# One decode step of a transformer block, forward and backward: q kept as rows, a fifth V tile, and the last head up to d(o) in another order

## The chip, the cores and the metric

The kernel runs on one core of a Trainium2 chip. The core has a matrix engine (PE), a vector engine (DVE), a scalar engine (ACT), a general engine (POOL), a sync engine (SP) and 16 DMA engines that move data between the device memory (HBM) and the on-chip memory (SBUF, 128 partitions; matmul results go to PSUM). The metric is the time of one execution on the device in microseconds (us); a kernel's figure is the median of its runs.

## The reference, cut

Inputs are bf16. One token x (1 x 640) goes through an attention block with a cache of 8192 keys and values for each of 32 heads (head size 192), and then through an MLP; both blocks are modulated by a condition c. The kernel must give the output and the gradients with respect to x, k_cache, v_cache, wq, wo, w3, w4, c and w_mod.

```python
def A(x, k_cache, v_cache, wq, wo):
    q = (x @ wq).reshape(1, 1, 32, 192).transpose(0, 2, 1, 3)
    scores = einsum('bhqd,bhkd->bhqk', q, k_cache) * 192 ** -0.5
    p = softmax(scores)
    o = einsum('bhqk,bhkd->bhqd', p, v_cache)
    return o.transpose(0, 2, 1, 3).reshape(1, 1, 6144) @ wo
def B(x, w1, w2, w3, w4):
...
    x1 = x + hs
    return x1 + gelu(layernorm(x1) @ w3) @ w4
sa, ca, ga, sb, cb, gb = (silu(c) @ w_mod).reshape(6, 640)
h = layernorm(x) * (1 + ca) + sa
x = x + ga * A(h, k_cache, v_cache, wq, wo)
h = layernorm(x) * (1 + cb) + sb
out = x + gb * B(h, w1, w2, w3, w4)
```

With a sequence of one token, hs (a mixer over shifted positions) is zero, so B is the MLP with its residual. k_cache and v_cache are 32 x 8192 x 192 each, that is 3 MB per head and cache; their gradients dK and dV have the same size. In the backward pass, d(o) is the gradient at the attention's output of each head; dV is p times d(o), and dK is dS times q, where dS = p * (V·d(o) - a constant of the head).

## The kernel before, in words

**Data.** A half head of K or V is one tile of 128 partitions x 32 positions x 192 (1536 KB). There are five K tiles, with names KX, KY, KC, KD, KE for the last ones in use (L348 to L353), and three V tiles, VB (L321). The queue of SP issues the loads: `load_k` L360, `load_v` L324, `load_w` L195 (wq and w_mod), `load_wo` L200 (one pair of heads of wo, 480 KB), `load_rows` L652 (rows of w4). The queue of POOL issues the stores. The order of the instructions on PE, DVE, ACT and SP is the order in which the program writes them (`manual_schedule`, L515 and L986).

**First phase, L516 to L600: heads 0 to 30, pipelined.** The vector q of every head, broadcast over the partitions and scaled, stands in one tile `qs_bc` (128 x 6144, L252). For head i, DVE multiplies K by q (L330) and adds the halves of the product (L334), PE sums the rest with identity matmuls (`dot_tree` L336), DVE reduces to the scores S (L344); then softmax (L365, E is the exponential), and E times V into tiles `vs` of a quarter head (L380 on DVE, L387 on ACT; three buffers). PE makes M = K-transposed times (E V), from which the gradient of q comes later, and the sums of o, in quarters (`m_quarter` L417, its units in `m_units` L396: 16 "main" matmuls for the first 128 columns of K and 16 "rest" for the other 64). For each pair of heads, `pair_sums` L471, `pair_o` L479 and `pair_ao` L488 make the pair's share of the attention output.

**Between the phases, L605 to L956.** An order written out by hand: the scores of the last head 31 (`score_mul`, `score_tree`), o of head 30 (`o_rows` L424, 64 matmuls) and the four quarters of its M between other work (`vs_act` L647, `vs_dve` L638 for E V), the last two pairs, the second layernorm by six sums (`S6` L766, two rsqrt L772 and L785, `n2_bf` L790), u = n2 w3 (`ups` L821), the gelu and its derivative, `du_bf` L869. In the same stretch PE transposes w3 in nine groups (`w3t` L813; a PSUM buffer of two, an ACT copy L808 each), and wo of the last pair in two (`do_t` L899, copies L895). Then `h2` L905 (g w4), `dn_ps` L916 (du w3T), `pr` L935, four means, and `dao_bf` L953, the gradient at the attention's output. The rows of w4 are in `w4b` and in `KX` (loads L666, L730, L765); the first six rows of the gradient of w4 are staged in KX (L934, L955) and stored from there (L956). `vs3`, the quarter of E V for the last M quarter, is made on ACT alone.

**Second phase, from L978: 64 half heads, from head 31 down.** `do_mm` L1011 makes `do_r`, d(o) of a head (matmuls with the transposed wo, then an ACT activation L1021). For each half head s, DVE multiplies V by d(o) (`mul_q` L1036), PE sums (`tree_q` L1051), DVE makes dS, PE and ACT make dV (`dv_groups` L1058, with E rows from `load_er` L990), and DVE makes dK = dS times q (`dk_part` L1070, with q as a slice of qs_bc, L1365). Both are stored. The V tiles come from a ring `v_buf` L1290; the load of half head s + 4 is issued in step s (L1405). The output tiles come from a ring `OB` L354. Beside it run the gradients of wq, wo, w_mod and w3 (`g_dq`, `g_dwo`, `g_wm`, `g_dw3`), in slots between the steps.

```python
353:    KX, KY, KC, KD, KE = (KB[(2 * HQ + k) % NKB] for k in (-4, -5, -3, -2, -1))
354:    OB = (KC, VB[2], KX, KE, KD)
1028:    wo_l[TL - 1] = load_wo(TL - 1)
1029:    er_l = {0: load_er(0, nc.sync), 1: load_er(1, nc.sync)}
1291:        return KY if s == 0 else VB[2] if s == 1 else (VB[1], KY, VB[0])[s % 3]
1365:        qh = qs_bc[:, h * DH : (h + 1) * DH]
1404:        if 0 < s < NS - 4:
1405:            v_l[s + 4] = load_v(*ht(s + 4), v_buf(s + 4))
```

## Time and profile before

| | before |
|---|---|
| median of 3 runs | 1406.0 us (1405.18 to 1406.44) |
| profiled execution, device time | 1404.99 us |
| its span (first to last instruction) | 1403.2 us |
| PE busy | 1182.8 us (84%), 12680 matmuls |
| DVE busy | 1111.0 us (79%) |
| ACT busy | 903.2 us (64%) |
| POOL busy | 104.9 us (7%) |
| DMA | 569.36 MB, mean 406 GB/s |
| mean granted clock of PE | 0.722 |

The profile of one execution is a page with the busy time of each engine, the span in 40 equal slices (each digit is the busy share of a slice in tenths, 9 is 90% or more), the DMA queues, the groups of instructions and the chain of work that ended last. Further views cut a stretch of time into windows (busy time of each engine, number of instructions in brackets, the clock that PE was granted, the share of time in which the 16 DMA engines were busy, and GB/s), or list the instructions of one engine in order of time (start, length, line, operation, what is written from what is read, and in brackets the idle time just before and what ended it). A line such as "L1072 DVE ... VB<-qs_bc,dS" is line 1072 of the kernel, on DVE, writing a VB tile from qs_bc and dS. The largest groups are the tree sums of V·d(o) on PE (L1056, 379.9 us), the copies of dV on ACT (L1068, 321.5 us with output tiles among the K tiles) and E V on ACT (L387, 303.6 us); 60% of the DMA time is on the queue of SP and 38.5% on that of POOL.

### The profile page before, as it was taken

To read this page: it belongs to the slowest core of one execution; us is meant where nothing else is said; L and a number is where in the kernel's file an instruction comes from. 1 tells how busy PE (TensorE), PEld (TensorE's weight loads), DVE (VectorE), ACT (ScalarE), POOL (GpSimd) and SP (SyncE) were. 2 spreads that over 40 slices of the span, in tenths; PEclk is the share of its full clock that TensorE was granted. 3 is DMA by queue.
4 is the path that set the end of the run, shared out by engine and by line. 5 is a ranking of instruction groups with operands and counts; after the bars stand their busy time and mean duration, and the time that the engine had idled before them with its cause. 6 is when DMAs were issued, how large, how long until landed. Compare 5 with 4: busy or idle time off the path is not lost.

```text
span 1403.2 us, 30406 instructions
## 1 busy us (share of the span) xinstructions
PE 1182.8 (84%) x12680; PEld 744.5 (53%) x12680; DVE 1111.0 (79%) x1460; ACT 903.2 (64%) x1972; POOL 104.9 (7%) x190
## 2 busy tenths in 40 slices
PE   3889889999998999899867987888989788779975
PEld 2777777777777778543323443434444344334421
DVE  4989899999999998976765875776766777868775
ACT  0777777777777778666554665665656476546654
POOL 0000000000000000110110110101110111101110
PEclk9999999999999999655555555555555565555555
DMA  9999999999999997699999999999999999999998
GB/s 375 401 417 419 415 417 423 407 424 409 422 414 415 408 413 306 223 394 425 423 396 421 423 422 421 421 424 422 425 418 425 423 413 423 421 412 398 426 379 367
DMA packets 76184, 569.36 MB, mean 406 GB/s; under 512 B 7278, under 2 KB 25022, under 8 KB 35982
## 3 DMA queue, kind: packets, MB, share of 16 engines
q1 hardware_dynamic: 51162, 342.03, 59.8%
q0 software_dynamic: 24368, 224.87, 38.5%
q8 instruction: 99, 1.62, 0.4%
q10 hardware_dynamic: 516, 0.51, 0.1%
q14 instruction: 39, 0.32, 0.1%
HBM read 340.95 MB, written 226.43 MB: 404 GB/s over the span
## 4 chain that ended last, share of the span: by engine, by line
issue 42%; DVE 21%; DMA 17%; PE 11%; POOL 5%; ACT 1%; SPq 0%; POOLq 0%; DVEq 0%
DMA KB<-in_A_k_cache_dram 10%; DVE prod L330 8%; DVE prod L334 4%; PE mp L402 3%; DMA out_dram<-KB 3%; DVE vs L380 2%; POOL out_dram L1322 2%; PE half_ps L340 2%; POOL out_dram L1318 2%; DMA w_st<-in_A_wq_dram 2%; PE mp L407 2%; DVE pq L1037 2%; DMA wo_st<-in_A_wo_dram 1%; PE dot_ps L1056 1%; DMA out_dram<-VB 1%
## 5 line engine op out<-in xcount | busy, mean ns | idle before, releaser
L1056 PE MATMUL dot_ps<-pq,ident_bf 128*128 128x256 bf16 x1494 | 379.9, 397 | 18.4 <-DVE dP L344 16.3
L1068 ACT CAST KB<-dv_ps 128x768 bf16<-128x768 f32 x416 | 321.5, 803 | 108.6 <-PE dv_ps L1067 106.3
L387 ACT ACTIVATE vs<-VB,Ef 128x192 bf16<-128x192 bf16 x840 | 303.6, 447 | 0.0
L1072 DVE TENSOR_TENSOR KB<-qs_bc,dS 128x3072 bf16<-128x3072 bf16 x98 | 169.4, 1753 | 103.5 <-DMA out_dram<-KB 91.8
L1056 PEld LDWEIGHTS <-ident_bf 128*128 128x128 bf16 x1494 | 150.1, 124 | 173.4 <-issue 134.3
L1067 PE MATMUL dv_ps<-do_r,er_b 1*128 1x192 bf16 x2048 | 230.3, 337 | 4.3 <-ACT KB L1068 2.9
L330 DVE TENSOR_TENSOR prod<-KB,qs_bc 128x6144 bf16<-128x6144 bf16 x62 | 207.9, 3353 | 28.1 <-DMA KB<-in_A_k_cache_dram 21.5
L402 PE MATMUL mp<-vs,KB 128*128 128x193 bf16 x1984 | 189.3, 247 | 4.6 <-ACT vs L387 3.4
L402 PEld LDWEIGHTS <-KB 128*128 128x128 bf16 x1984 | 169.0, 97 | 13.6 <-DMA KB<-in_A_k_cache_dram 5.3
L895 ACT COPY wT<-wT_ps 128x1024 bf16<-128x1024 bf16 x82 | 79.0, 964 | 128.7 <-PE wT_ps L894 128.5
L1037 DVE TENSOR_TENSOR pq<-VB,do_r 128x3072 bf16<-128x3072 bf16 x86 | 150.5, 1749 | 12.7 <-PE dot_ps L1056 12.7
L1067 PEld LDWEIGHTS <-er_b 1*128 1x128 bf16 x2048 | 69.3, 104 | 154.8 <-issue 152.2
L340 PE MATMUL half_ps<-prod,ident_bf 128*128 128x256 bf16 x744 | 95.1, 279 | 45.7 <-DVE prod L334 45.5
L380 DVE TENSOR_TENSOR vs<-VB,E 128x1728 bf16<-128x1728 bf16 x120 | 123.7, 1052 | 0.3 <-ACT vs L387 0.3
L334 DVE TENSOR_TENSOR prod<-prod 128x3072 bf16<-128x3072 bf16 x62 | 108.8, 1754 | 1.0
L340 PEld LDWEIGHTS <-ident_bf 128*128 128x128 bf16 x744 | 73.0, 99 | 64.1 <-issue 55.0
L407 PE MATMUL mp<-vs,KB 128*64 128x193 bf16 x1976 | 106.5, 250 | 0.0
L1068 ACT CAST VB<-dv_ps 128x768 bf16<-128x768 f32 x96 | 75.1, 802 | 39.3 <-PE dv_ps L1067 39.1
L367 ACT ACTIVATE E<-S_h,negm 128x256 bf16<-128x256 f32 x31 | 15.8, 508 | 116.9 <-DVE negm L538 114.6
L407 PEld LDWEIGHTS <-KB 128*64 128x64 bf16 x1976 | 79.4, 110 | 19.8 <-issue 19.5
L344 DVE TENSOR_REDUCE dP<-dot_ps 128x32 f32<-128x512 f32 x64 | 44.0, 687 | 57.8 <-PE dot_ps L1056 57.6
L1072 DVE TENSOR_TENSOR VB<-qs_bc,dS 128x3072 bf16<-128x3072 bf16 x30 | 51.5, 1753 | 29.5 <-DMA out_dram<-VB 24.8
(360 smaller groups left out, 1132.7 us busy)
## 6 DMA issues: line engine op xcount, KB each, us to landing
VB<-in_A_v_cache_dram SPq DMA_DIRECT2D x103, 1536.0 KB
out_dram<-KB POOLq DMA_DIRECT2D x99, 1536.0 KB, 16.2
KB<-in_A_k_cache_dram SPq DMA_DIRECT2D x64, 1536.0 KB
...
```

The costliest lines, as they stand in the source:

```text
L330: V_.tensor_tensor(out=prod, in0=src, in1=vec[:, None, :].to_broadcast([P, JH, DH]), op=ALU.mult)
L334: V_.tensor_tensor(out=prod[:, :, 0:HW], in0=prod[:, :, 0:HW], in1=prod[:, :, DH - HW : DH], op=ALU.add)
L340: T_.matmul(ps, lhsT=ident_bf, rhs=prod[:, :, k : k + TF], start=(k == 0), stop=(k == w - TF))
L380: V_.tensor_tensor(out=vs[:, 0:n, 0:DH].rearrange("p j (a b) -> p j a b", b=4), in0=v[:, v0 : v0 + n, :].rearrange("p j (a b) -> p j a b", ...
L387: A_.activation(out=vs[:, k, 0:DH], in_=v[:, v0 + k, :], func=ACT.Copy, scale=Ef[:, j0 + k : j0 + k + 1])
L402: T_.matmul(mp[:, 0:MW], lhsT=kb[:, j0 + k, 0:P], rhs=vs[:, k, 0:MW], start=(q == 0 and k == 0), stop=(z and k == JQ - 1), skip_group_chec ...
L407: T_.matmul(mp[p0 : p0 + 64, MO : MO + MW], lhsT=kb[:, j0 + k, P:DH], rhs=vs[:, k, 0:MW], start=False, stop=(z and k >= JQ - 2), skip_grou ...
L1037: V_.tensor_tensor(out=pq[:, q], in0=v_l[s][:, q * JQ : (q + 1) * JQ, :], in1=do_of(ht(s)[0])[:, None, :].to_broadcast([P, JQ, DH]), op=AL ...
L1056: T_.matmul(ps[:, q * JQ : (q + 1) * JQ, :], lhsT=ident_bf, rhs=pq[:, q, :, k : k + TS], start=(k == 0), stop=(k == w - TS), skip_group_ch ...
L1067: T_.matmul(ps[:, b, k * DH : (k + 1) * DH], lhsT=er[p0 : p0 + 1, 2 * m + k, :], rhs=doh[p0 : p0 + 1, :], start=True, stop=True)
L1068: A_.copy(out=dV4[:, 2 * q : 2 * q + 2, m * PW : (m + 1) * PW], in_=ps[:, :, 0:PW])
L1072: V_.tensor_tensor(out=dK[:, lo:hi, :].rearrange("p j (a b) -> p j a b", b=4), in0=qh.rearrange("p (a b) -> p a b", b=4)[:, None, :, :].to ...
```

## The change

**q as rows.** At head 28, POOL's queue stores row 0 of qs_bc (all heads' q, 12 KB) to a DRAM tile `q_d`, and at head 30 loads it back as `q_rows`, 32 rows x 192. In the second phase, a new function `q_bc(h)` broadcasts one row with a one-hot matmul into PSUM and copies it to a small tile `qh` on ACT: once before the loop for head 31, and then at the end of each head's last step for the next head. The tile qs_bc is free after the last head's scores. It then holds rows 4 to 12 of w4 (one load instead of two into KX), stages the first six rows of w4's gradient, and takes KX's place in the ring of output tiles (as `QT`).

**A fifth V tile.** KX becomes a V tile: half head 4 of the second phase is loaded into it (`v4`) after the rest of M quarter 1. The ring `v_buf` has four tiles, and step s issues the load of half head s + 5.

**The last head up to d(o) in another order.** `o_rows` of head 30 is split around the row maximum of the last scores. The matmuls of pair 14 (`pair_ao`) and the load of the last row block of w3 go behind the exponential. All of vs2 is made on ACT; vs3 is made on ACT (0 to 8) and DVE (8 to 16, behind du). `m_main` and `m_rest` take the place of m_units. The first w3 transposes come behind u's matmuls. The M quarters stand at other places in the order; the second half of quarter 3 comes behind `pr`, with `m_add` of head 30 behind `dao_bf`.

**wo ahead of h2.** `do_t` of the last pair comes before h2's matmuls; its result goes to the tile of w3's last row block (`w3_w`) instead of a part of KC. The load of wo for pair 14 goes from before the loads of E's rows to behind the second `do_mm`. The copy of h2 to `bo` and the first six gradient rows of w4 go behind `dao_bf`: three on ACT, three on DVE. A few small temporary tiles now share buffers (tag "rows").

The diff, without context (the hunks that only give the small tiles the shared tag are left out):

```diff
...
@@ -252,0 +253,3 @@
+QT = qs_bc.rearrange("p (j d) -> p j d", d=DH)
+q_rows = const.tile([HQ, DH], BF16, name="q_rows")
+q_d = dram.tile([HQ, DH], BF16, name="q_d")
@@ -354 +357 @@
-OB = (KC, VB[2], KX, KE, KD)
+OB = (KC, VB[2], QT, KE, KD)
@@ -410,0 +414,5 @@
+def m_main(q, kb, vs, mp, lo, hi):
+    j0 = (q % 2) * JQ
+    for k in range(lo, hi):
+        T_.matmul(mp[:, 0:MW], lhsT=kb[:, j0 + k, 0:P], rhs=vs[:, k, 0:MW], start=(q == 0 and k == 0), stop=(q == 3 and k == JQ - 1), skip_group_check=True)
@@ -424 +432 @@
-def o_rows(h, v2, op):
+def o_rows(h, v2, op, lo=0, hi=J):
@@ -426 +434 @@
-    for j in range(J):
+    for j in range(lo, hi):
@@ -586,0 +595,4 @@
+        if i == H1 - 3:
+            nc.gpsimd.dma_start(out=q_d.rearrange("h d -> (h d)").rearrange("(o n) -> o n", o=1), in_=qs_bc[0:1, :])
+        if i == H1 - 1:
+            nc.gpsimd.dma_start(out=q_rows, in_=q_d)
@@ -679,2 +690,0 @@
-    op_y = psO.tile([P, 256], FP32, name="op")
-    o_rows(H1 - 1, vy, op_y)
@@ -689,0 +700,2 @@
+    op_y = psO.tile([P, 256], FP32, name="op")
+    o_rows(H1 - 1, vy, op_y, 0, JH)
@@ -690,0 +703,2 @@
+    mx = row_max(x["S"])
+    o_rows(H1 - 1, vy, op_y, JH, J)
@@ -694,8 +707,0 @@
-    ps_ao = pair_ao(o2, wo_l.pop(TL - 1), psB, "b")
-    w3_4 = wst.tile([P, F], BF16, name="w3_4", tag="wo")
-    nc.sync.dma_start(out=w3_4, in_=w3d[:, 4, :])
-    V_.tensor_copy(out=AO[:, :, 2 * TL - 2 : 2 * TL], in_=ps_ao)
-    pe = m_units(0, ky[0], vs0, mp)
-    pe.pop(0)()
-    mx = row_max(x["S"])
-    pe.pop(0)()
@@ -707,2 +712,0 @@
-    A_.activation(out=zy, in_=es0, func=ACT.Copy, scale=32.0)
-    A_.copy(out=oy, in_=op_y[:, 0:DH])
@@ -710,0 +715,7 @@
+    A_.activation(out=zy, in_=es0, func=ACT.Copy, scale=32.0)
+    A_.copy(out=oy, in_=op_y[:, 0:DH])
+    ps_ao = pair_ao(o2, wo_l.pop(TL - 1), psB, "b")
+    w3_w = wst.tile([P, 3 * D], BF16, name="w3_w", tag="wo")
+    w3_4 = w3_w[:, 0:F]
+    nc.sync.dma_start(out=w3_4, in_=w3d[:, 4, :])
+    load_rows(qs_bc[:, 0 : 8 * D], 4, 12)
@@ -712,0 +724 @@
+    vs_dve(vs1, 1, 0, JQ // 2)
@@ -716 +727,0 @@
-    vs_dve(vs1, 1, 0, JQ // 2)
@@ -717,0 +729 @@
+    V_.tensor_copy(out=AO[:, :, 2 * TL - 2 : 2 * TL], in_=ps_ao)
@@ -719,3 +731 @@
-    vs_act(vs2, 2, JQ // 2, JQ // 2 + 3)
-    vs_dve(vs2, 2, 0, JQ // 2)
-    pe.pop(0)()
+    vs_act(vs2, 2, 0, 2)
@@ -723 +733 @@
-    vs_act(vs2, 2, JQ // 2 + 3, JQ)
+    vs_act(vs2, 2, 2, 12)
@@ -726 +735,0 @@
-    m_rest(0, ky[0], vs0, mp, JQ // 2, 13)
@@ -729,2 +738 @@
-    m_rest(0, ky[0], vs0, mp, 13, JQ)
-    load_rows(flat(KX)[:, 0 : 4 * D], 4, 8)
+    m_main(0, ky[0], vs0, mp, 0, 5)
@@ -746,5 +754 @@
-    vs3 = new_vs(3)
-    vs_act(vs3, 3, 0, 8)
-    pe = m_units(1, ky[0], vs1, mp)
-    pe.pop(0)()
-    pe.pop(0)()
+    m_main(0, ky[0], vs0, mp, 5, JQ)
@@ -763,3 +767,4 @@
-    pe.pop(0)()
-    pe.pop(0)()
-    load_rows(flat(KX)[:, JQ * DH : JQ * DH + 4 * D], 8, 12)
+    m_rest(0, ky[0], vs0, mp, 0, JQ)
+    m_main(1, ky[0], vs1, mp, 0, JQ)
+    m_rest(1, ky[0], vs1, mp, 0, JQ)
+    v4 = load_v(H1 - 2, 0, KX)
@@ -781 +786,3 @@
-    vs_act(vs3, 3, 8, 10)
+    vs_act(vs2, 2, 12, JQ)
+    vs3 = new_vs(3)
+    vs_act(vs3, 3, 0, 2)
@@ -817,4 +823,0 @@
-    w3t()
-    pe = m_units(2, ky[1], vs2, mp)
-    pe.pop(0)()
-    pe.pop(0)()
@@ -830 +833 @@
-    vs_act(vs3, 3, 10, 14)
+    w3t()
@@ -850,3 +853 @@
-    vs_act(vs3, 3, 14, JQ)
-    pe.pop(0)()
-    pe.pop(0)()
+    m_main(2, ky[1], vs2, mp, 0, 8)
@@ -853,0 +855,2 @@
+    m_main(2, ky[1], vs2, mp, 8, JQ)
+    vs_act(vs3, 3, 2, 8)
@@ -855,2 +858 @@
-    pe = m_units(3, ky[1], vs3, mp)
-    pe.pop(0)()
+    m_rest(2, ky[1], vs2, mp, 0, JQ)
@@ -859 +860,0 @@
-    pe.pop(0)()
@@ -871 +872 @@
-    pe.pop(0)()
+    m_main(3, ky[1], vs3, mp, 0, 8)
@@ -873 +874 @@
-    pe.pop(0)()
+    m_rest(3, ky[1], vs3, mp, 0, 8)
@@ -875 +875,0 @@
-    mt = mp_out(H1 - 1, mp)
@@ -901 +901 @@
-            woT[t] = flat(KC)[:, JQ * DH : JQ * DH + 3 * D] if t == TL else bst.tile([P, 15 * P], BF16, name="wT", tag="wT")
+            woT[t] = w3_w if t == TL else bst.tile([P, 15 * P], BF16, name="wT", tag="wT")
@@ -905,4 +904,0 @@
-    h2_ps = psB.tile([P, 512], FP32, name="h2_ps", tag="b")
-    for k in range(ND):
-        for a in range(NF):
-            T_.matmul(h2_ps[:, k : k + 1], lhsT=w4r(a)[:, k * P : (k + 1) * P], rhs=g_bf[:, a : a + 1], start=(a == 0), stop=(a == NF - 1))
@@ -910,0 +907,8 @@
+    h2_ps = psB.tile([P, 512], FP32, name="h2_ps", tag="b")
+    def h2_part(lo, hi):
+        for k in range(lo, hi):
+            for a in range(NF):
+                T_.matmul(h2_ps[:, k : k + 1], lhsT=w4r(a)[:, k * P : (k + 1) * P], rhs=g_bf[:, a : a + 1], start=(a == 0), stop=(a == NF - 1))
+    h2_part(0, ND)
@@ -921 +925 @@
-    m_add(H1 - 1, mp, mt)
+    vs_dve(vs3, 3, 8, JQ)
@@ -933,5 +936,0 @@
-    V_.tensor_copy(out=bo, in_=h2_ps[:, 0:ND])
-    dw4_dve(flat(KX), 0, 0, 3)
-    pr = col(4 * ND, "pr").rearrange("p (a b) -> p a b", b=ND)
-    V_.tensor_tensor(out=pr, in0=dn_ps[:, None, :].to_broadcast([P, 4, ND]), in1=G, op=ALU.mult)
-    ps = mean_mm(pr.rearrange("p a b -> p (a b)"), 4 * ND)
@@ -943,0 +943,7 @@
+    V_.tensor_tensor(out=Bg, in0=B1, in1=ga, op=ALU.mult)
+    pr = col(4 * ND, "pr").rearrange("p (a b) -> p a b", b=ND)
+    V_.tensor_tensor(out=pr, in0=dn_ps[:, None, :].to_broadcast([P, 4, ND]), in1=G, op=ALU.mult)
+    ps = mean_mm(pr.rearrange("p a b -> p (a b)"), 4 * ND)
+    m_main(3, ky[1], vs3, mp, 8, JQ)
+    m_rest(3, ky[1], vs3, mp, 8, JQ)
+    mt = mp_out(H1 - 1, mp)
@@ -946 +951,0 @@
-    V_.tensor_tensor(out=Bg, in0=B1, in1=ga, op=ALU.mult)
@@ -955,2 +960,5 @@
-    dw4_dve(flat(KX), 0, 3, 6)
-    dw4_store(flat(KX), 0, 6)
+    V_.tensor_copy(out=bo, in_=h2_ps[:, 0:ND])
+    dw4_act(qs_bc, 0, 0, 3)
+    dw4_dve(qs_bc, 0, 3, 6)
+    m_add(H1 - 1, mp, mt)
+    dw4_store(qs_bc, 0, 6)
@@ -1028 +1035,0 @@
-wo_l[TL - 1] = load_wo(TL - 1)
@@ -1069,0 +1077,7 @@
+def q_bc(h):
+    ps = psB.tile([P, 512], FP32, name="q_ps", tag="b")
+    T_.matmul(ps[:, 0:DH], lhsT=pick(HQ, h), rhs=q_rows, start=True, stop=True)
+    qh = bst.tile([P, DH], BF16, name="qh", bufs=2)
+    A_.copy(out=qh, in_=ps[:, 0:DH])
+    return qh
...
@@ -1291 +1305 @@
-return KY if s == 0 else VB[2] if s == 1 else (VB[1], KY, VB[0])[s % 3]
+return KY if s == 0 else VB[2] if s == 1 else (VB[0], VB[1], KX, KY)[(s - 2) % 4]
@@ -1295 +1309,2 @@
-v_l = {s: v_buf(s) for s in range(4)}
+v_l = {s: v_buf(s) for s in range(5)}
+assert ht(4) == (H1 - 2, 0) and v_buf(4) is KX
@@ -1331,0 +1347 @@
+wo_l[TL - 1] = load_wo(TL - 1)
@@ -1334 +1350 @@
-v_l[4] = load_v(*ht(4), v_buf(4))
+v_l[5] = load_v(*ht(5), v_buf(5))
@@ -1358,0 +1375 @@
+qh = q_bc(H1)
@@ -1365 +1381,0 @@
-qh = qs_bc[:, h * DH : (h + 1) * DH]
@@ -1404,2 +1420,2 @@
-if 0 < s < NS - 4:
-    v_l[s + 4] = load_v(*ht(s + 4), v_buf(s + 4))
+if 0 < s < NS - 5:
+    v_l[s + 5] = load_v(*ht(s + 5), v_buf(s + 5))
@@ -1444,0 +1461,2 @@
+if nxt and ht(s + 1)[0] != h:
+    qh = q_bc(ht(s + 1)[0])
```

## The prediction

> **What bounds the kernel now.** All times are us from the start of the one profiled execution: span 1403.2, device time 1404.99, so 1.8 lies around the span; the median of the runs is 1406.0, 1.0 above it. I read the 40 slices first, and then the hole they show in windows of 5 us (columns: length, busy time of PE, PEld, DVE, ACT, POOL, granted PE clock, DMA share, GB/s).
>
> ```profile
> DMA  9999999999999997699999999999999999999998
> 0.00:540.00 540.00, 473.91 (x7239) 396.17 (x7240) 494.73 (x500) 384.10 (x1248) 8.77 (x22) 1.00 1.01 412
> 590.00:1360.00 770.00, 641.81 (x4649) 306.25 (x4646) 546.90 (x804) 460.32 (x619) 87.54 (x153) 0.54 1.01 416
> 550.00:555.00 5.00, 5.00 (x56) 4.61 (x55) 3.60 (x22) 3.46 (x12) 0.00 (x0) 0.74 0.49 143
> 555.00:560.00 5.00, 3.98 (x103) 3.63 (x102) 4.81 (x27) 4.20 (x12) 0.67 (x2) 1.00 0.33 120
> 560.00:565.00 5.00, 4.84 (x86) 4.25 (x84) 4.83 (x11) 4.79 (x8) 0.39 (x1) 1.00 0.05 16
> 565.00:570.00 5.00, 3.87 (x123) 3.68 (x119) 4.59 (x30) 2.77 (x5) 0.00 (x0) 0.96 0.33 103
> 570.00:575.00 5.00, 3.31 (x23) 2.05 (x24) 4.32 (x10) 2.82 (x5) 0.84 (x1) 0.50 0.38 137
> 575.00:580.00 5.00, 4.75 (x32) 2.30 (x32) 4.90 (x7) 2.51 (x4) 0.55 (x1) 0.50 0.69 220
> 580.00:585.00 5.00, 4.72 (x28) 3.14 (x23) 4.96 (x9) 4.77 (x7) 0.54 (x1) 0.50 0.96 330
> 585.00:590.00 5.00, 4.01 (x62) 2.40 (x59) 4.96 (x5) 3.43 (x6) 1.38 (x2) 0.83 0.81 304
> ```
>
> The 16 DMA engines are full up to 540 and from 590 to 1360 (share 1.01). What they leave unused from 550 to 590 is 5 x (0.51 + 0.67 + 0.95 + 0.67 + 0.62 + 0.31 + 0.04 + 0.19) = 19.8 us: no buffer is free to load into, and nothing can be stored before d(o) exists. So the span is transfer work plus this hole plus some 4 us at the tail. The bytes stay (q as rows adds 2 x 12 KB), so an edit is worth what it does to the hole: a later d(o) lengthens it, a transfer moved into it shortens what follows. The path through it is then read from the timelines of ACT and DVE (start, length, and in brackets the idle time before and its releaser).
>
> ```profile
> 552.78 0.29 ACT L150 ACTIVATE ln_lnv<-sc,eps_c 128x1 f32<-128x1 f32 x1 [1.34 <-DVE sc L771]
> 562.90 2.51 ACT L808 COPY KB<-w3T_ps 128x1024 bf16<-128x1024 bf16 x3 [0.21 <-PE w3T_ps L807]
> 565.29 0.34 ACT L444 COPY M<-mp 128x193 f32<-128x193 f32 x1
> 566.64 1.82 ACT L895 COPY KB<-wT_ps 128x1024 bf16<-128x1024 bf16 x2 [0.68 <-PE wT_ps L894]
> 571.59 0.42 ACT L1021 ACTIVATE do_r<-do_ps,rinv 128x192 bf16<-128x192 f32 x1 [3.13 <-PE do_ps L1018]
> 581.62 4.42 ACT L914 ACTIVATE stg<-w4b,g__10304 128x640 bf16<-128x640 bf16 x6
> 566.01 0.17 DVE L869 SCALAR_TENSOR_TENSOR du_bf<-t__10307,d_g 128x12 bf16<-128x12 f32 x1
> 568.52 0.17 DVE L936 TENSOR_TENSOR pr<-dn_ps,G 128x20 f32<-128x20 f32 x1
> 572.04 1.76 DVE L1037 TENSOR_TENSOR pq<-KB,do_r 128x3072 bf16<-128x3072 bf16 x1 [0.57 <-ACT do_r L1021]
> 582.71 3.42 DVE L1072 TENSOR_TENSOR VB<-qs_bc,dS 128x3072 bf16<-128x3072 bf16 x2
> ```
>
> The reader is to see three places: ACT is done with the w3T copies when du arrives; ACT stands idle for 3.13 us before do_r, so nothing is ahead of it; the first dK (582.71) reads qs_bc without waiting, while ACT is in the six w4 gradient rows.
>
> **The change, part by part.** *The fifth V tile* (1536 KB = 1.57 MB) is issued where the second part of w4's rows went, behind M quarter 1 at about 554, into idle engines. At 420 GB/s it is 3.7 us that no longer follow: -3.7; bounds -3.7 and 0 (if the last steps, then free of loads one step sooner, are held by compute: DVE was 19.05 of 20 us busy at 1340 to 1360). I take -3.7, since a store's landing still holds DVE for 7.74 us at 1332. The w4 rows move ahead into the full stretch, which then ends 1.6 us later: 0. The load of wo for pair 14 goes behind d(o): 480 KB, 1.2 us, into unused time at 575 to 590: 0; +1.2 without that.
>
> *Scores and pair sums.* The 64 o rows (1.50 at 536.42) go behind the score tree, which waits for DVE at 537.4 instead: last score sum at 540.75 for 541.96 (-1.2). The o copy is 1.2 earlier, so are rinv and the second ao. Then the mean of six sums has 11 M matmuls before it (1.0 at full clock) and no longer quarter 1 (16 in 2.69 at the half clock of 549.5 to 552): S at 550.15 behind the dot product on DVE, for 552.11: -2.0.
>
> *Up to u.* Between the two rsqrt ACT now has 4 + 2 scalings and a copy (6 x 0.365 + 0.2 = 2.4) for 2 (0.78): n2 at 554.2 for 554.7, -0.5. DVE's work to u is unchanged; exp waits behind the first w3T copy, which has moved behind u's matmuls: du_bf -0.5 (565.6).
>
> *w3T, wo, h2.* This is the step that decides. ACT idles from 554.1 to 556.5 for the first copy. The fourth copy writes into vs2's buffer, so it waits until quarter 2's rest is read; that now comes behind the fifth transposes: 561.0. Behind it on ACT stand six vs3 scalings (2.2), then copies five to nine (0.96, 0.5, 0.96, 0.96, 0.5 by the row of three): 568.2 for 565.4. PE has wo's transposes next, and their second group needs the ninth copy's PSUM buffer: 568.2 + 0.45; only then h2 (60 matmuls, 1.5) and dn (60, 1.5): 571.65. Before, h2 ran at 564.5 while ACT copied, and dn ended at 568.4. So pr is +3.2. DVE alone would have been ready at 565.6 + 2.9 (eight vs3 rows 0.97, fourteen small operations 1.9): 568.5. Bounds for pr: 0 (DVE sets it) and +3.2; I take +3.2, as every wait in it is a buffer's reader.
>
> *d(o).* pr to dao_bf stays 2.0: 573.7. The second half of quarter 3 stands on PE ahead of d(o)'s matmuls: 8 + 8 at the half clock seen from 570 on (0.168 and 0.107 each) 2.2, at full clock 1.3: d(o)'s matmuls from 574.4 or 573.8. On ACT, ahead of do_r, now stand two M copies (0.66) and three w4 gradient rows (3 x 0.737 = 2.2), which wait for quarter 3: do_r at 577.3 or 576.4 for 571.59. So +5.7 or +4.8 in all; I take +5.3. DVE's m_add is behind dao_bf and three rows; the load of E's rows on SP waits for it (about 575.5), and wo and the next V queue behind that load; before, it was issued at 568.40 and its user started at 572.06, so at most 3.7 later: 579.2 against do_r's 577.7, 0 to +1.5, and only for PE's dV: 0. The queue of POOL gains a store and a load of q between stores of E at heads 28 and 30: 0.
>
> *q as rows.* 32 matmuls and 32 ACT copies of 192 columns (0.32 by the dq row's copy) lie beside transfers: 0; +0.6 in the two last heads without them. But the first copy stands behind the six w4 rows (4.42) on ACT, and the first dK needs it: 586.04 + 0.35 for 582.71, so DVE stalls 3.7 there, with the second dK, the next products, dP and the V load behind it; the DMA share around is 0.81, so no queue of transfers covers it: +3.7 (0 if one does).
>
> **Sum.** -3.7 + 5.3 + 3.7 = +5.3: span 1408.5, and against the median 1406.0 + 5.3 = 1411.3.
>
> The Trainium skill (TensorE: Matmul & The Clock Gate, "The HAM clock gate") says that PE falls to half clock after an idle window of about 3.4 us. The trace has a half-clock stretch of 3 us at 549.5 and a lasting one from 570, after stretches of one-column matmuls more than after idle time; by the rule, PE's waits for ACT at 561 to 568 could halve the clock there already, which is the third rival.
>
> **The rivals.** (1) *Faster: ACT keeps pace.* If copies and matmuls overlap so that the 2.0 won at S lasts to du, dn runs at once (pr -1.5, as DVE's part to pr is 0.5 longer), do_r comes 0.8 later through the gradient rows alone, and the first dK's stall falls under transfers that the additional tile leaves queued: 0.8 - 3.7 = -2.9, 1403.1. For: ACT's 3.13 us and 1.34 us idle. Against: the vs2 buffer, and a share of 0.05 at 560 to 565 with nothing queued. It decides once do_r's delay and the stall together are under 0.9. (2) *No change: DVE sets dn.* pr 0, do_r +2.2, stall +3.7, tile -3.7: +2.2, 1408.2. For: DVE is 4.8 of 5 us busy there. Against: PE's order, do_t ahead of h2. (3) *Slower still: PE is cold from 563 on, or the tail keeps the tile.* At half clock wT's 15 transposes take 1.95 for 0.83 (8 in 1.04 at 591.5), h2 and dn some 0.6 more each (15 one-column ones in 0.58 at 1336): +2.3, 1413.6; without the tile's return +3.7, 1415.0. (4) *The tile isn't early:* its load stands on SP behind the load into qs_bc; if that had to wait for d(o), +3.7 as well. It waits for q's store at head 28 only, so 0.03.
>
> **How the numbers follow.** Forecast 0.50, rival 1 0.17, rival 2 0.18, rivals 3 and 4 0.15. About 0.2% (2.8 us) can be told from no change. Slower takes the forecast but for 0.03 of it, and rivals 3 and 4: 0.62; same is rival 2 and that 0.03: 0.21; faster 0.17. The forecast's own range is 1408 to 1414; to hold 8 in 10 it reaches down over rival 2 to rival 1's 1403.1 and up to rival 3's 1415.
>
> **What would show it.** The tile: a V load at about 554, and the share at 555 to 560 near 0.9. Early part: S near 550. w3T: the ninth copy at about 568 and dn's end at 571 to 572; if dn ends before 569.5, that step is wrong. d(o): two M copies and three gradient rows directly before do_r, do_r at 576 to 578. q: the first dK held by qh for about 3.7 us. The whole is wrong if do_r comes before 573 or the first dK doesn't wait, or if full transfer engines don't make a later start into a later end.

## The result, and the profile after

| | median, us | before on the same chip | ratio (95% interval) | profiled execution |
|---|---|---|---|---|
| changed kernel, 8 runs | 1412.43 | 1406.16 | 1.0054 (1.0036 to 1.0071) | 1421.4 |
| changed kernel again, 12 runs | 1413.38 | 1406.34 | 1.0045 (1.0029 to 1.0060) | 1412.63 |

The change makes the kernel slower by 0.45 to 0.54%, that is 6.3 to 7.6 us. The profiled execution of the first row was the slowest of its eight (1421.4), so all lines of the changed kernel below are from the second row's (span 1410.8).

The 40 slices of that profile. The two slices of the hole, 6 and 9 tenths before ("7699"), are now lower:

```profile
DMA  9999999999999997589999999999999999999998
```

The hole in windows of 5 and 10 us; the columns are those of the prediction's windows (length, PE, PEld, DVE, ACT, POOL, PE clock, DMA share, GB/s):

```profile
550.00:555.00 5.00, 3.44 (x94) 3.03 (x91) 3.40 (x17) 2.41 (x8) 0.00 (x0) 0.99 0.80 277
555.00:560.00 5.00, 4.70 (x52) 4.42 (x51) 4.74 (x20) 2.08 (x6) 1.07 (x2) 0.66 0.23 93
560.00:565.00 5.00, 1.64 (x22) 1.34 (x19) 4.83 (x17) 4.59 (x10) 0.00 (x0) 1.00 0.00 0
565.00:570.00 5.00, 5.00 (x84) 4.50 (x82) 0.95 (x9) 3.72 (x5) 0.00 (x0) 0.66 0.01 3
570.00:575.00 5.00, 4.73 (x103) 3.99 (x99) 2.15 (x12) 0.59 (x1) 0.00 (x0) 0.70 0.02 3
575.00:580.00 5.00, 2.41 (x20) 1.70 (x18) 1.85 (x3) 4.20 (x8) 0.86 (x1) 0.50 0.06 20
580.00:585.00 5.00, 4.13 (x27) 1.52 (x25) 4.86 (x8) 3.23 (x5) 0.55 (x1) 0.50 1.03 319
585.00:590.00 5.00, 4.72 (x31) 3.21 (x28) 4.27 (x7) 4.04 (x6) 0.54 (x1) 0.50 0.92 300
590.00:600.00 10.00, 5.19 (x62) 3.05 (x60) 7.16 (x6) 4.58 (x8) 1.39 (x2) 0.67 0.85 353
```

What the transfer engines leave unused is 5 x (0.20 + 0.77 + 1.00 + 0.99 + 0.98 + 0.94 + 0 + 0.08) + 10 x 0.15 = 26.3 us, for 19.8 before. The tile's load fills 0.80 of the first window, and then almost nothing moves until 580 (shares of 0.00 to 0.06 from 560 on). Two things stand out on PE: it is busy for only 1.64 us at 560 to 565, and its clock is down to 0.66 on both sides of that.

The path through the hole, from the timelines of SP, ACT and DVE of the same execution (the first line is the load of the fifth V tile):

```profile
550.71 0.33 SPq L328 DMA_DIRECT2D KB<-in_A_v_cache_dram  x1
560.20 1.01 ACT L815 COPY vs<-w3T_ps 128x1024 bf16<-128x1024 bf16 x1 [3.12 <-PE mp L423]
561.11 2.18 ACT L662 ACTIVATE vs<-VB,Ef 128x192 bf16<-128x192 bf16 x6
563.19 1.47 ACT L815 COPY vs<-w3T_ps 128x1024 bf16<-128x1024 bf16 x2
567.92 0.59 ACT L815 COPY KB<-w3T_ps 128x512 bf16<-128x512 bf16 x1 [0.32 <-PE w3T_ps L814]
575.14 0.32 ACT L452 COPY M<-mp 128x193 f32<-128x193 f32 x1 [4.55 <-PE mp L423]
575.48 0.32 ACT L454 COPY mt<-mp 64x193 f32<-64x193 f32 x1
575.82 2.26 ACT L918 ACTIVATE qs_bc<-w4b,g__10287 128x640 bf16<-128x640 bf16 x3
578.11 0.42 ACT L1029 ACTIVATE do_r<-do_ps,rinv 128x192 bf16<-128x192 f32 x1
572.14 0.18 DVE L945 TENSOR_TENSOR pr<-dn_ps,G 128x20 f32<-128x20 f32 x1 [6.16 <-PE dn_ps L923]
592.80 3.43 DVE L1086 TENSOR_TENSOR VB<-qh,dS 128x3072 bf16<-128x3072 bf16 x2 [3.49 <-ACT qh L1081]
```

Three waits were not there before: the fourth w3T copy waits 3.12 us for M quarter 2 to be read, pr waits 6.16 us on DVE for dn (0 before), and the first dK waits 3.49 us for qh. Before do_r, where ACT had idled for 3.13 us, it now makes two M copies and three gradient rows (2.9 us), and only after a wait of 4.55 us for quarter 3.

Starts counted from the last V load of the first phase, so that what went on before the hole drops out (before: 534.06, changed: 531.60), with the forecast's steps and three of the experiments below (each column is one profiled execution):

| us after that load | before | forecast | changed | six scalings earlier | all mended | old order, tile kept |
|---|---|---|---|---|---|---|
| row maximum negated (negm) | 9.48 | 8.3 | 8.47 | 8.26 | 8.74 | 9.48 |
| S of the layernorm | 18.05 | 16.1 | 16.25 | 15.95 | 16.45 | 16.97 |
| du_bf | 31.95 | 31.5 | 31.56 | 31.28 | 31.77 | 30.85 |
| pr | 34.46 | 37.7 | 40.54 | 37.19 | 36.33 | 33.37 |
| do_r | 37.53 | 42.8 | 46.51 | 43.15 | 38.50 | 36.36 |
| first dK | 48.65 | 57.7 | 61.20 | 57.84 | 49.62 | 47.48 |

### The profile page after: what moved, and what is told of

It reads as the page before. It is cut to its first block, busy times and chain, and to the rows that moved or that the text cites. A ratio compares the mean times of both kernels' runs of the same rounds, so it can differ in the third digit from the quotient of the medians.

```text
span 1419.6 us, 30487 instructions
## 1 busy us (share of the span) xinstructions
PE 1200.5 (85%) x12712; PEld 752.5 (53%) x12712; DVE 1110.7 (78%) x1457; ACT 914.8 (64%) x2007; POOL 106.4 (7%) x192
## 4 chain that ended last, share of the span: by engine, by line
issue 47%; POOL 6%; DVE 2%; ACT 1%; DMA 1%; PE 1%; POOLq 0%; ACTq 0%; DVEq 0%
POOL out_dram L1337 2%; POOL out_dram L1333 2%; DMA out_dram<-VB 1%; DVE pq L1044 1%; POOL out_dram L1176 1%; POOL out_dram L1203 1%; PE dot_ps L1063 1%; ACT KB L1075 0%; DVE VB L1086 0%; PE dv_ps L1074 0%; ACT stg L918 0%; DVE pq L1056 0%; DVE KB L1086 0%; ACT qs_bc L918 0%; POOL out_dram L1235 0%
## 5 line engine op out<-in xcount | busy, mean ns | idle before, releaser
L1063 PE MATMUL dot_ps<-pq,ident_bf 128*128 128x256 bf16 x1494 | 383.9, 401 | 26.8 <-DVE dP L347 23.5
L1075 ACT CAST KB<-dv_ps 128x768 bf16<-128x768 f32 x312 | 241.9, 804 | 82.9 <-PE dv_ps L1074 81.2
L405 PE MATMUL mp<-vs,KB 128*128 128x193 bf16 x1920 | 184.4, 248 | 3.5 <-ACT vs L390 3.3
L405 PEld LDWEIGHTS <-KB 128*128 128x128 bf16 x1920 | 165.0, 98 | 12.6 <-DMA KB<-in_A_k_cache_dram 4.3
L1086 DVE TENSOR_TENSOR KB<-qh,dS 128x3072 bf16<-128x3072 bf16 x74 | 127.8, 1753 | 55.2 <-DMA out_dram<-KB 46.5
L1044 DVE TENSOR_TENSOR pq<-VB,do_r 128x3072 bf16<-128x3072 bf16 x66 | 115.5, 1750 | 8.5 <-PE dot_ps L1063 8.5
L1044 DVE TENSOR_TENSOR pq<-KB,do_r 128x3072 bf16<-128x3072 bf16 x62 | 108.5, 1750 | 8.6 <-PE dot_ps L1063 6.4
L410 PE MATMUL mp<-vs,KB 128*64 128x193 bf16 x1920 | 102.9, 250 | 0.0
L1075 ACT CAST qs_bc<-dv_ps 128x768 bf16<-128x768 f32 x104 | 80.5, 804 | 28.1 <-PE dv_ps L1074 27.6
## 6 DMA issues: line engine op xcount, KB each, us to landing
out_dram<-VB POOLq DMA_DIRECT2D x26, 1536.0 KB, 15.2
```

What stands on the lines that cost most here:

```text
L405: T_.matmul(mp[:, 0:MW], lhsT=kb[:, j0 + k, 0:P], rhs=vs[:, k, 0:MW], start=(q == 0 and k == 0), stop=(z and k == JQ - 1), skip_group_chec ...
L410: T_.matmul(mp[p0 : p0 + 64, MO : MO + MW], lhsT=kb[:, j0 + k, P:DH], rhs=vs[:, k, 0:MW], start=False, stop=(z and k >= JQ - 2), skip_grou ...
L1044: V_.tensor_tensor(out=pq[:, q], in0=v_l[s][:, q * JQ : (q + 1) * JQ, :], in1=do_of(ht(s)[0])[:, None, :].to_broadcast([P, JQ, DH]), op=AL ...
L1063: T_.matmul(ps[:, q * JQ : (q + 1) * JQ, :], lhsT=ident_bf, rhs=pq[:, q, :, k : k + TS], start=(k == 0), stop=(k == w - TS), skip_group_ch ...
L1075: A_.copy(out=dV4[:, 2 * q : 2 * q + 2, m * PW : (m + 1) * PW], in_=ps[:, :, 0:PW])
L1086: V_.tensor_tensor(out=dK[:, lo:hi, :].rearrange("p j (a b) -> p j a b", b=4), in0=qh.rearrange("p (a b) -> p a b", b=4)[:, None, :, :].to ...
```

## The experiments

Each ratio is against the kernel before on the same chip. Differences between kernels are differences of ratios, times 1407 us. A ratio has a 95% interval of some ±0.0015, so such a difference is known to about ±3 us; what a single step is worth is therefore read from times and timelines together. A range such as 2.4 to 3.7 comes from the two rows of the changed kernel in the table of results.

**The second profile of the changed kernel** (its lines are above).

> The changed kernel itself, again, beside the next three. Its first profile was its slowest execution (1421.4 us; the others lay from 1410.3 to 1417.1), with the last scores 1.7 us later than before and do_r 12.0 us later. If that execution was an odd one: negm of the last head at 538 to 541 us and do_r at 576 to 578, ratio 1.0054 within its interval. Rival (it is typical, and the sum of the prediction hides a larger loss paid back elsewhere): negm at 545 and do_r at 583 again.

Measured: 1.0045, span 1410.8. What follows: the loss is there again.

**q copied ahead of the six gradient rows.**

```diff
@@ in the second phase, before the loop
+qh = q_bc(H1)
 dw4_act(stg0, 6, 6, 12)
-qh = q_bc(H1)
```

> The changed kernel with one move: the matmul and the copy that make qh of head 31 stand ahead of the six w4 gradient rows on ACT instead of behind them. The prediction's third term (the first dK waits for qh): the stall of 3.48 us at the first dK is gone, the first dK follows the second product at once, and since no full DMA queue covers it the median falls by 3 to 3.7 us, to a ratio of about 1.0030 against the kernel before (1.0054 for the changed kernel). Rival (the stall is hidden, since the fifth V tile is already loaded and the stores behind can catch up): the stall is gone in the trace, but the ratio stays at 1.0054 within its interval.

Measured: 1.0028 (1.0016 to 1.0040), 2.4 to 3.7 us below the changed kernel. The first dK starts 11.12 us after do_r, exactly as before the change, for 14.69 in the changed kernel; in this kernel's timeline of DVE it waits for nothing:

```profile
587.48 1.75 DVE L1086 TENSOR_TENSOR VB<-qh,dS 128x3072 bf16<-128x3072 bf16 x1
```

What follows: the stall is one line's place, and it costs time; by the two measurements of the changed kernel together 2.9 us, give or take 2.3, so it is not hidden behind queued transfers.

**The three gradient rows of ACT on DVE, where it waits for dn.**

```diff
+dw4_dve(qs_bc, 0, 0, 3)
 pr = col(4 * ND, "pr")...
...
-dw4_act(qs_bc, 0, 0, 3)
 dw4_dve(qs_bc, 0, 3, 6)
```

> The changed kernel with the first three gradient rows of w4 back on DVE ahead of pr, where DVE waited 6.33 us for dn. The prediction's second term, its ACT part: do_r comes right behind the matmuls of d(o) and the two M copies, about 2.0 us earlier after dao_bf (4.4 us lay between them in the changed kernel's trace, 1.25 in the one before), and the median falls by 1.5 to 2.2 us, ratio about 1.0040. Rival (do_r waits for the second half of quarter 3 on PE anyway): the distance from dao_bf to do_r stays above 3.5 us and the ratio stays.

Measured: 1.0069 (1.0056 to 1.0081): slower than the changed kernel, by 2.1 to 3.4 us, where 1.5 to 2.2 us less was expected. do_r does come 2.58 us behind dao_bf instead of 4.43, but the second do_mm starts 8.3 us behind it instead of 5.66, since PE's dV stands in front of it. The timelines of POOL, SP and PE show why:

```profile
573.58 0.86 POOL L883 DMA_DIRECT2D out_dram<-qs_bc  x1 [17.40 <-DVE qs_bc L880]
574.66 1.90 SPq L1003 DMA_DIRECT2D er_b<-eT_d  x2
579.65 0.66 PE L1074 MATMUL dv_ps<-do_r,er_b 1*128 1x192 bf16 x6 [5.25 <-DVE pq L1044]
```

The store of the six gradient rows (960 KB) is issued 1.1 us ahead of the load of E's rows (two of 8 KB), and that load's first user starts 5.0 us after its issue. PE's row puts this wait down to DVE's pq, a product of which ended at 579.55; but these matmuls read only do_r, ready since 575.1, and E's rows (er_b). That it is the load they wait for is read from that, and the next two kernels test it.

**The store moved behind the dV store, with the same rows on DVE.**

```diff
-dw4_store(qs_bc, 0, 6)
...
 dv_store(0, dV0, 0, JQ)
+dw4_store(qs_bc, 0, 6)
```

> The changed kernel with three gradient rows of w4 on DVE ahead of pr, as in e2_rows_dve, and the store of the six rows issued behind the first store of dV instead of directly. Theory: in e2_rows_dve do_r came early, but the load of E's rows was issued 1.1 us behind that store of 0.98 MB, shared the DMA engines with it, and came 5.0 us after its issue instead of 2.3; so with the store held back the first dV matmuls follow do_r within 0.8 us, do_mm of the second head with them, and the ratio falls from 1.0069 to about 1.0040 (1.5 to 2 us below the changed kernel). Rival (what holds dV there is not the store): the first dV matmuls stay 4 to 5 us behind the issue of E's rows, ratio about 1.007.

Measured: 1.0060 (1.0039 to 1.0081). Inconclusive: POOL issued the store at 574.05, 1.49 us behind dao_bf, just as in the kernel with the rows on DVE alone. The order that the program fixes is that of PE, DVE, ACT and SP; POOL is not among them, so the edit did not move the store.

**E's rows loaded ahead of the store: m_add of head 30 ahead of the last three gradient rows.**

```diff
+dw4_dve(qs_bc, 0, 0, 3)
 pr = col(4 * ND, "pr")...
...
 V_.tensor_copy(out=bo, in_=h2_ps[:, 0:ND])
-dw4_act(qs_bc, 0, 0, 3)
+m_add(H1 - 1, mp, mt)
 dw4_dve(qs_bc, 0, 3, 6)
-m_add(H1 - 1, mp, mt)
 dw4_store(qs_bc, 0, 6)
```

> e2_rows_dve with m_add ahead of the three gradient rows on DVE, so that the load of E's rows, which waits for m_add, is issued ahead of the store of the six rows, which waits for the rows (e5_store_late did not do this: POOL issued the store at the same place as before, 574.05). Theory: in e2_rows_dve the load came 5.0 us after its issue since the store of 0.98 MB was 1.1 us ahead of it; here the first dV matmuls follow the issue of E's rows by 2.3 to 3 us, the second do_mm comes 2.5 to 4 us earlier relative to dao_bf than in e2_rows_dve (8.3), and the ratio falls from 1.0069 to 1.003 to 1.0045. Rival (dV waits for something else): 8.3 us and a ratio of 1.006 to 1.007 again.

Measured: 1.0041 (1.0028 to 1.0054), 3.9 us below the kernel with the rows on DVE alone. Now the load is issued 1.24 us ahead of the store, and its first user starts 2.8 us after it, released by the load itself:

```profile
575.61 1.12 SPq L1003 DMA_DIRECT2D er_b<-eT_d  x2
576.85 0.86 POOL L883 DMA_DIRECT2D out_dram<-qs_bc  x1 [19.87 <-DVE dq_x L1312]
578.39 0.68 PE L1074 MATMUL dv_ps<-do_r,er_b 1*128 1x192 bf16 x8 [3.06 <-DMA er_b<-eT_d]
```

What follows: the order of that load and that store is worth about what was lost. Against the changed kernel nothing is won that can be told (1.0045 to 1.0054): in this profile u's matmuls start 1.1 us later, since the 16 matmuls of quarter 1 ahead of them take 2.77 us at half clock, for 1.52 in the profile of the changed kernel. The two kernels are the same up to there, so this is a difference between executions.

**Six vs3 scalings ahead of the fourth w3T copy.**

```diff
 m_main(2, ky[1], vs2, mp, 0, 8)
+vs_act(vs3, 3, 2, 8)
 w3t()
 m_main(2, ky[1], vs2, mp, 8, JQ)
-vs_act(vs3, 3, 2, 8)
```

> The changed kernel with the six vs3 scalings (2.18 us on ACT) ahead of the fourth w3T copy, in ACT's wait of 3.30 us for the buffer of vs2, instead of behind it. The prediction's step on w3T: copies five to nine come 2.2 us earlier, so dn ends about 2.2 us earlier, do_r with it, and the median falls by about 2 us, ratio about 1.0040. Rival (DVE sets dn): DVE ended its own work 6.3 us before pr in the one trace, so it would have to be PE's clock that made the difference there; then dn's end moves by less than 0.7 us.

Measured: 1.0028 (1.0015 to 1.0041), 2.4 to 3.7 us below the changed kernel; from the V load to pr 37.19 us for 40.54, a gain of 3.4. The scalings themselves are 2.2. The timelines of ACT and PE of this kernel:

```profile
555.19 2.21 ACT L662 ACTIVATE vs<-VB,Ef 128x192 bf16<-128x192 bf16 x6
558.45 2.42 ACT L815 COPY vs<-w3T_ps 128x1024 bf16<-128x1024 bf16 x3 [1.05 <-PE mp L423]
561.07 2.62 ACT L815 COPY KB<-w3T_ps 128x1024 bf16<-128x1024 bf16 x3 [0.20 <-PE w3T_ps L814]
553.92 1.50 PE L417 MATMUL mp<-vs,KB 128*128 128x193 bf16 x8
560.87 0.84 PE L417 MATMUL mp<-vs,KB 128*128 128x193 bf16 x8
563.25 1.04 PE L894 MATMUL wT_ps<-ident_bf,wo_st 128*128 128x128 bf16 x15 [0.32 <-ACT KB L815]
```

And PE of the changed kernel, the same instructions:

```profile
555.68 1.50 PE L417 MATMUL mp<-vs,KB 128*128 128x193 bf16 x8
564.24 0.38 PE L814 MATMUL w3T_ps<-ident_bf,wp 128*128 128x128 bf16 x4 [2.59 <-ACT vs L815]
564.68 1.02 PE L417 MATMUL mp<-vs,KB 128*128 128x193 bf16 x8
567.67 1.45 PE L894 MATMUL wT_ps<-ident_bf,wo_st 128*128 128x128 bf16 x15
```

The windows view of both, first this kernel and then the changed one; the third column from the right is PE's clock:

```profile
562.00:564.00 2.00, 1.68 (x28) 1.33 (x26) 1.96 (x14) 1.69 (x4) 0.00 (x0) 1.00 0.00 0
564.00:566.00 2.00, 2.00 (x81) 2.00 (x79) 0.21 (x2) 1.72 (x2) 0.00 (x0) 1.00 0.03 8
```

```profile
564.00:566.00 2.00, 1.76 (x21) 1.74 (x21) 1.91 (x15) 1.68 (x3) 0.00 (x0) 0.80 0.00 0
566.00:568.00 2.00, 2.00 (x22) 1.53 (x20) 0.00 (x0) 1.09 (x2) 0.00 (x0) 0.50 0.00 0
```

With the scalings out of its way PE no longer waits 2.59 us for a copy, its clock stays at full speed to 566, eight M matmuls take 0.84 instead of 1.02 and wo's 15 transposes 1.04 instead of 1.45, and the six copies from the fourth to the ninth run almost without a gap: 5.24 us from the start of the fourth to the end of the ninth, for 8.31. So the six scalings cost 2.2 us by themselves and 0.9 more through PE's wait and its clock. That the wait brings the half clock is borne out by the other profiles: the seven that have the wait of 2.59 us all have half clock from 0.4 to 1.3 us behind its end, and the two kernels with the scalings ahead (this one and the one with all steps mended) have none there. The first half-clock stretch stays: eight M matmuls of quarter 2 take 1.50 in both kernels.

**No fifth V tile.**

```diff
-v4 = load_v(H1 - 2, 0, KX)
...
-return KY if s == 0 else VB[2] if s == 1 else (VB[0], VB[1], KX, KY)[(s - 2) % 4]
+return KY if s == 0 else VB[2] if s == 1 else (VB[1], KY, VB[0])[s % 3]
...
-    v_l[s + 5] = load_v(*ht(s + 5), v_buf(s + 5))
+    v_l[s + 4] = load_v(*ht(s + 4), v_buf(s + 4))
```

> The changed kernel without the fifth V tile: no early load into KX, the ring of three of before, loads four half heads ahead; all else as changed. The prediction's first term: one transfer of 1.57 MB comes behind d(o) instead of ahead of it, the DMA share at 550 to 560 falls back to about 0.4, and the median rises by 3.7 us, ratio about 1.0080. Rival (the tile is not worth its transfer, since the steps behind d(o) are held by PE at half clock and not by transfers): the ratio stays within 1 us of the changed kernel's, 1.0054.

Measured: 1.0092 (1.0078 to 1.0105), 5.3 to 6.6 us above the changed kernel. In its windows the DMA share at 550 to 560 falls below the 0.4 that was expected:

```profile
550.00:555.00 5.00, 3.80 (x98) 3.35 (x97) 3.41 (x15) 2.42 (x9) 0.00 (x0) 1.00 0.23 77
555.00:560.00 5.00, 4.35 (x42) 4.08 (x40) 4.71 (x26) 2.85 (x6) 1.07 (x2) 0.66 0.04 13
```

What follows: the tile is worth something, and the forecast's 3.7 lies within the noise of this difference; it is priced a second time below.

**All of it mended, in the new order.** Beside the two moves of the kernels with q ahead and with the scalings earlier, the other vs2 and vs3 scalings of ACT stand behind the second rsqrt, vs3 of DVE ahead of the gelu's derivative, h2 and the whole of quarter 3 amid the last three w3T groups, and m_add, the copy of h2 and three gradient rows (on DVE) ahead of pr.

```diff
+h2_part(0, 3)
 w3t()
+h2_part(3, 5)
 ...
+m_main(3, ky[1], vs3, mp, 8, JQ)
 ...
+m_rest(3, ky[1], vs3, mp, 8, JQ)
+mt = mp_out(H1 - 1, mp)
...
+m_add(H1 - 1, mp, mt)
+V_.tensor_copy(out=bo, in_=h2_ps[:, 0:ND])
+dw4_dve(qs_bc, 0, 0, 3)
 pr = col(4 * ND, "pr")...
...
-dw4_act(qs_bc, 0, 0, 3)
```

> The changed kernel with all its steps behind u mended: the second rsqrt ahead of six scalings, vs3's scalings in ACT's wait, vs3's second half on DVE ahead of the dot products with w4, the whole quarter 3 and h2 amid the w3T groups, m_add and three gradient rows on DVE ahead of pr, qh of head 31 ahead of the six rows. By the prediction's steps: n2 0.6 to 1.5 us earlier than in e3_vs3_early, dn's end 2 to 3 earlier, do_r directly behind d(o) (1.3 us after dao_bf instead of 4.4), the first dK 11.1 us behind do_r instead of 14.7: the first dK 8 to 10 us earlier than in e3_vs3_early, ratio 0.996 to 0.998, faster than the kernel before. Rival (the transfers behind the hole, not its length, set the end): the first dK comes early but the ratio stays above 1.000.

Measured: 1400.91 us, 0.9951 (0.9932 to 0.9970): faster than both. do_r comes 38.50 us after the V load (532.37) and the first dK 49.62: 8.0 and 11.6 less than in the changed kernel. The lines of ACT and DVE:

```profile
570.87 0.42 ACT L1030 ACTIVATE do_r<-do_ps,rinv 128x192 bf16<-128x192 f32 x1 [2.06 <-PE do_ps L1027]
581.99 1.75 DVE L1087 TENSOR_TENSOR VB<-qh,dS 128x3072 bf16<-128x3072 bf16 x1
```

What follows: the delays of the new order can be taken back almost wholly. That the kernel is faster than the one before does not show a gain of the new order; the last experiment gives as much without it.

**The tile and q as rows in the old order.** The kernel before, with q_d, q_rows and q_bc (called early), qs_bc among the output tiles, the fifth V tile, and the shared tag; the last head, the M quarters and wo stand where they stood before.

```diff
-OB = (KC, VB[2], KX, KE, KD)
+OB = (KC, VB[2], QT, KE, KD)
...
+load_rows(qs_bc[:, 0 : 8 * D], 4, 12)
...
+v4 = load_v(H1 - 2, 0, KX)
...
+qh = q_bc(H1)
```

> The kernel before with only q as rows (qh of head 31 ahead of the six w4 gradient rows), w4's rows in qs_bc and the fifth V tile; the last head and the way to d(o) in the old order. The prediction's first term by itself: do_r where it was (28 us behind negm), one V load at about 554, the median 3.7 us lower, 1402.4, ratio 0.9974. Rival (the tile returns nothing, since the first steps behind d(o) are held by compute): ratio 0.9995 to 1.0005. Second rival (the queue of loads one tile ahead takes DMA time from the first stores): ratio above 1.0005.

Measured: 1398.63 us, 0.9946 (0.9929 to 0.9963): faster than both. Its timelines of ACT and DVE have do_r 36.36 us after the V load (530.54), and the first dK 11.12 us behind that:

```profile
566.90 0.42 ACT L1028 ACTIVATE do_r<-do_ps,rinv 128x192 bf16<-128x192 f32 x1 [3.06 <-PE do_ps L1025]
578.02 1.75 DVE L1086 TENSOR_TENSOR VB<-qh,dS 128x3072 bf16<-128x3072 bf16 x1
```

What follows: the reordering and the late place of qh are more than the whole loss. The changed kernel is 13.9 to 15.2 us slower than the same change without them. The expected 0.9974 was missed, too: the gain is about twice the 3.7 us of the tile, and the next runs look for the rest.

**The same without the fifth tile.**

```diff
-v4 = load_v(H1 - 2, 0, KX)
...
-    v_l[s + 5] = load_v(*ht(s + 5), v_buf(s + 5))
+    v_l[s + 4] = load_v(*ht(s + 4), v_buf(s + 4))
```

> e7_tile_only without the fifth V tile: q as rows, w4's rows and the w4 gradient rows in qs_bc, qh early, but the ring of three V tiles and loads four half heads ahead, as before. In e7_tile_only the median fell by 7.6 us (ratio 0.9946) where the prediction's term for the tile is 3.7. Theory A (the tile is worth about 7 us, as e4_four_v says too, which lost 5.3): ratio here 0.999 to 1.001. Theory B (the tile is worth its transfer, 3.7, and the other half comes from w4's rows being loaded at once and ahead, out of the way): ratio here about 0.9972. In both, the DMA share at 550 to 560 is below 0.45.

Measured: 1402.35 us, 0.9970 (0.9957 to 0.9983). So the tile is worth 0.0024 x 1407 = 3.4 us in the old order, give or take 3. But what is left, q as rows without a tile and without a new order, is itself 4.2 us faster than before, where it was forecast at 0. That was unexplained.

**The kernel before, profiled again** beside these two.

> The kernel before itself, for a second profile. Its first one has the last V load of the first phase at 534.06 and negm at 543.54; seven of eight profiles of the other kernels have them at 529.6 to 532.4 and 538.4 to 541.1. If the first phase is the same for all kernels and only differs between executions or chips: V load at 530 to 532 here too, do_r 37.5 us behind it. Rival (something in the change makes the first phase 2 to 4 us shorter): 534 again.

Measured: 1406.51 us, span 1404.7, do_r 37.71 us after the V load, the first dK 11.12 behind it. What follows: the profile of before is a fair one.

**Only the layout of the small tiles.** The changed kernels all give some small tiles one shared buffer and have q_rows, and with that the large tiles behind them in SBUF start at other bytes: the first K tile at 143360 instead of 144256 in each partition, the first V tile at 94208 instead of 95104. This kernel is the one before with these two things alone; q_rows is never read.

```diff
-rows = tmp.tile([NF, P], BF16, name="bc_rows")
+rows = tmp.tile([NF, P], BF16, name="bc_rows", tag="rows")
...
+q_rows = const.tile([HQ, DH], BF16, name="q_rows")
+V_.memset(q_rows, 0.0)
```

> The kernel before with nothing changed but where its tiles lie: the small temporary tiles share the tag rows (as in the change) and a tile q_rows is set to zero and never read. That moves the K tiles and V tiles 896 bytes down in each partition, to where the changed kernel has them (first K tile at byte 143360, a multiple of 4096, instead of 144256; first V tile at 94208 instead of 95104). Theory (the rest of what e8_rows_only gained is the place of the tiles: transfers of the first phase run about 0.7% faster in all kernels with this layout): the last V load of the first phase at 530 to 532 instead of 534, ratio 0.997 to 0.9985. Rival (the gain comes from w4's rows being loaded at once, or from q): V load at 534, ratio 0.9995 to 1.0005.

Measured: 1400.16 us, 0.9945 (0.9926 to 0.9965): an edit that moves no instruction of the kernel's work, and adds only one memset and the shared buffers, gives 7.7 us, more than its theory asked for (0.997 to 0.9985). The windows view over the full stretch, of before and of this kernel, shows a part of it; the last two columns are the DMA share and GB/s:

```profile
100.00:540.00 440.00, 403.00 (x6252) 339.53 (x6252) 417.64 (x416) 332.02 (x1083) 7.01 (x13) 1.00 1.01 415
```

```profile
100.00:540.00 440.00, 406.57 (x6320) 342.46 (x6320) 418.20 (x425) 334.55 (x1093) 7.03 (x13) 1.00 1.01 419
```

The transfer engines are equally full and move 1% more. Both profiles of before have 415 GB/s here; the twelve of kernels with the new layout have 416 to 419, 417.7 in the mean, and the last V load comes at 529.27 in this kernel instead of 534.06 (531.2 in the mean of the twelve). The spread is wide: two of the twelve load no sooner or hardly sooner than before, the old order without the fifth tile (533.36) and the first profile of the changed kernel (534.49). And do_r comes 36.46 us after the load instead of 37.53: the half-clock stretch of PE at 549.5, in both profiles of before, is missing in this kernel and in the two with the old order; why is open (the last section has a candidate). So some 2.8 us of the 7.7, in the mean of the profiles, lie in the first phase and 1.1 in the hole; where the rest lies is not shown, as the profiled execution of this kernel was the slowest of its six, only 2.9 us below that of before.

One reading follows for all kernels above. The layout alone (0.9945), the old order with the tile (0.9946) and the new order mended (0.9951) can't be told apart. All three have the new layout, so against a kernel before with that layout neither the tile and q as rows nor the new order shows a gain. The tile's 3.4 us stand against 3.5 us, give or take 3.3, by which the kernel with q as rows and without the tile (0.9970) is slower than the layout alone.

The Trainium skill (DMA: Bandwidth & Descriptors, "How a descriptor splits into AXI transactions") says that when a descriptor does not start at a multiple of 256 bytes, its first transaction starts at the multiple below, and the bytes ahead of the start are fetched for nothing. If a row of a tile, 12288 bytes, is one descriptor, an estimate by that page is 388 beats instead of 384 for the old starts, which lie 128 above such a multiple (the new ones lie on it): 1.0%, where the measured difference is 0.6% in the mean and 1.0% for 415 and 419 GB/s. But the page tells this of reads, the tiles are what the loads of this stretch write, and no other offsets were run. So the place of the tiles is shown as the cause, and its alignment is not.

## Why the prediction was right in sum and wrong in two steps

The sum was close, 5.3 us for a measured 6.3 to 7.6, but that is luck in part: two errors of some 4 us cancel in it. By the rows above: order and stall, the first dK at 61.20 us after the V load in the changed kernel and 47.48 in the old order with the tile, +13.7 (13.9 to 15.2 in time); layout and q as rows, -4.2; the tile, -3.4. That makes +6.1. Forecast were +9.0, 0 and -3.7.

- *The hole sets the span.* Right in the main: the unused transfer time grew by 6.5 us. In these two executions the span grew by 7.6; the first phase was 2.5 us shorter, and what follows the hole some 3.6 longer (413 GB/s from 590 to 1360 for 416), which the forecast did not have and no run explains.
- *The fifth V tile, -3.7.* Right within the noise of ±3 us: -3.4 in the old order, -5.3 to -6.6 in the new one. Its load came at 550.71 instead of about 554, so the window that it fills is the one at 550 (0.80), and not the one at 555; the whole stretch was 2.5 us earlier.
- *Scores, S, n2 and du.* Right against the profile of before: -1.0 for -1.2 at the row maximum, -1.8 for -2.0 at S, -0.4 for -0.5 at du_bf. But 1.1 of the 1.8 at S comes without any reordering (16.97 in the old order with the tile, where the half-clock stretch at 549.5 is missing), and at du_bf that kernel, at 30.85, is 0.7 ahead of the changed one.
- *"w3T, wo, h2", +3.2 at pr.* This step failed in size: +6.1. Its mechanism is there as described, the fourth copy behind vs2's buffer, six scalings behind it and h2 behind wo's transposes. But each of its durations was taken at full clock. The fourth copy started 1.7 us later than forecast (28.60 for 26.9 after the V load), behind matmuls of quarter 2 at half clock, and the ninth ended 8.31 us later, not 7.2, as PE's wait for the scalings dropped the clock once more: 1.7 + 1.1 = 2.8, nearly the whole miss of 2.9. From the fourth to the ninth copy it is 8.0 to 8.7 us in all seven profiles with the scalings behind the fourth; the kernel with the scalings earlier shows this second part. The first part is clock as well: in the profile of the kernel with q ahead PE is at full clock there, eight matmuls of quarter 2 take 0.84, and the time from the first to the fourth copy is 4.63 us instead of 5.96. The third rival named a cold clock from 563 on as another outcome and priced it at 2.3. Of its terms only wo's transposes ran partly at half clock (1.45 for 1.00); h2 and dn took 3.1 us together as forecast.
- *d(o), +2.1 more.* It was +2.9, so do_r came +9.0 in all, for +5.3. The M copies wait for quarter 3's matmuls, which run at half clock, until 1.5 us behind dao_bf. The two copies and three rows stand before do_r as forecast.
- *The load of E's rows, "0 to +1.5, and only for PE's dV: 0".* Right in the changed kernel only because the gradient rows hold do_r back as long. With them gone, the load comes behind the store and costs more than it was given.
- *The stall at the first dK, +3.7.* Right: 3.49 in the row, 3.57 in the distance from do_r, and 2.4 to 3.7 us in the time (±2.3) when it is taken away.
- *q as rows and the shared tag, 0.* This step failed too: the forecast costed instructions and left out that tiles move. The layout alone gave 0.9945. Whether q's matmuls and copies cost something beside it stays open: with them, and without the tile, it is 0.9970 (0.9957 to 0.9983), and the intervals overlap.

Of the rivals, the faster one (ACT keeps pace) did not happen. The mended order, with the scalings, the rows and qh out of the way, takes 1400.91, but the layout alone takes 1400.16. In the mended kernel do_r is 2.1 us later than in the old order with the tile, and the two are the same in time (0.9951 and 0.9946), so nothing here shows a gain from the reordering. The second (DVE sets dn) is out, as DVE waited 6.16 us for dn, and so is the fourth, as the tile's load was issued at 550.71. The early part alone (1.0 at the row maximum) on top of the old order was not tried.
